# A sketched-attention and top-2 expert kernel: a router with other steps, one row tile for both halves of batch 0, and the first block's rows turned earlier in the program

## The chip, the cores and the metric

The kernel runs on one core of one Trainium2 chip. A core has TensorE (PE, whose weight loads the profile shows apart as PEld), VectorE (DVE), ScalarE (ACT), GpSimd (POOL) and SyncE (SP), each with a queue of its own that it works off in order. The metric is the device time of one execution in microseconds; the time of a kernel is the median of its runs. The kernel before took 388.87 us (three runs, 386.61 to 390.64).

## The reference

Four batches of 1088 tokens, four heads of 32, float32. A sketch turns every key and query head into 64 features, the attention is linear in them, and its result (4352 tokens by 128) goes through a noisy top-2 router to eight experts of 128 x 1024 x 128:

```python
a, b = x @ S1.T, x @ S2.T                  # 8 numbers each, per head and token
phi = outer(a, b).reshape(64)
kv, z = phi(k).T @ v, phi(k).sum(0)
x = (phi(q) @ kv) / (phi(q) @ z + 1e-6)    # heads side by side: (4352, 128)
noisy = x @ w_gate + log1p(exp(x @ w_noise)) * noise
top2 = the two largest of the 8 per token; w = softmax over the two
out = sum over the two of w * (relu(x @ w1[e]) @ w2[e])
```

## The kernel before, in words

**Stages.** A batch is eight tiles of 128 tokens; the 64 tokens left over of two batches share a ninth tile, so routers 0 to 3 have 8, 9, 8 and 9 tiles. `Features` makes the features of up to four tiles: `turn` transposes on PE and copies on ACT, `sketch` multiplies by the sketch on PE and has ACT copy one part out of PSUM, `multiply` adds the other part from PSUM (L363) and forms the outer product (L368), both on DVE, the product on POOL where that is asked for. `keys_values` (L404) sums keys times values in one PSUM bank, `through_router` (L418, L424) folds the router's weights in, `Attend` (L444, L461) gives numerators, denominators and raw logits in a tile `nd`.

**Router.** `router` (L471) is a generator of small DVE steps, one a `yield`: divide, add up the heads, softplus, noise, then twice over maximum, compare, rank, pick; then prefix sums over the tiles, and on PE three small matmuls (L561 to L563) count how many earlier tokens chose each expert. With the start of the expert's area (`base`) this gives the row `to` of each token's two copies. The token, times its weight, goes into a tile `xg` (L586), and one indirect DMA for each tile and choice (L603, POOL) scatters 128 rows of it to `xs` in DRAM. `xg` has two buffers. Batch 0 is routed as two halves, `h0` and `h1`, of four tiles, each with an `xg` of its own; their steps alternate on DVE, by the counts in `both(n)`.

**Blocks.** `table` works out on DVE which expert and which rows each block of 128 rows has (`making` in the code). `work_off` goes through 72 blocks: it fetches a block's weights (L750) and rows (L758) on SP, turns the rows on PE (L762), and multiplies by w1 (L816) and w2 (L773) in two halves; ACT or DVE applies the relu, POOL scatters the results (L780). Blocks come in waves of 9, 18, 16 and 29; a wave's rows can be fetched when its batch's scatters have landed. Within the waves each further half block is one `next` on the generator, and the work of later batches lies between them.

**What sets the order.** On PE, ACT and DVE the order is that of the program (`manual_schedule`). The orders of POOL and SP are set by the framework's scheduler, which places an instruction by when it believes it ready; so a step that stands later in the program can stand earlier there. `first_batches` writes the order up to the first blocks out by hand: batch 0 (tiles `k0`, `k1`, `kr`, `q0`, `q1`), batch 1's keys `l0`, `l1` and queries `p0`, `p1`, `pr`, batch 2's keys `m0`, `m1`, `mr`. Then come the steps of router 1, and between them batch 2's `keys_values`; the first `next` on the blocks is after `LONE` = 2 yields of `routing(1)`, which cover twelve router steps and half of batch 2's `keys_values`, and after six more steps and its other half.

Of the kernel before, what the change touches and what calls it, by code (L numbers as in the profile page):

```python
# [11 lines left out]
ALU = mybir.AluOpType  # L12
# [9 lines left out]
def kernel(  # L22
# [192 lines left out]
    base = const.tile([P, E], F32, name="base")  # L215
    for e in range(E):
        nc.gpsimd.memset(base[:, e:e + 1], float(e * CAP))
# [15 lines left out]

    carry = [const.tile([P, E], F32, name="carry0")]
    nc.gpsimd.memset(carry[0][:], 0.0)
# [94 lines left out]
    class Features:  # L330
# [14 lines left out]
        def sketch(self):  # L345
            n, ps = self.n, early_bank(self.b, self.stream)
            for i in range(n):
                nc.tensor.matmul(ps[:, P * i:P * (i + 1)], lhsT=self.xT[:, P * i:P * (i + 1)],  # L348
                                 rhs=sk[:].rearrange("p i h y -> p (i h y)"), start=True, stop=True)
            self.two = ps[:, 0:P * n].rearrange("p (a i b y) -> p a i b y", a=n, i=2, b=H)  # L350
            self.ab = work.tile([P, G, H, 2, R], F32, name="ab", tag=f"ab{self.stream}",
                                bufs=3 if self.stream == "k" else 2)
            self.o = self.ab[:, 0:n].rearrange(
                "p a b w r -> p b a (w r)" if self.by_head else "p a b w r -> p a b (w r)")
            nc.scalar.copy(self.o, self.two[:, :, 1])  # L355

        def multiply(self, engine=V):
            for _ in self.products(engine):
                pass

        def products(self, engine=V):
            n = self.n
            yield V.tensor_tensor(out=self.o, in0=self.two[:, :, 0], in1=self.o, op=ALU.add)  # L363
            if self.phi is None:
                self.phi = work.tile([P, G, H, RR], F32, name="phi", tag=f"phi{self.stream}",
                                     bufs=3 if self.stream == "q" else 2)
            th = self.ab[:, 0:n].rearrange("p t h w r -> p (t h) w r")
            yield engine.tensor_tensor(  # L368
                out=self.phi[:, 0:n].rearrange("p t h (i j) -> p (t h) i j", i=R),
                in0=th[:, :, 0, :].unsqueeze(3).to_broadcast([P, H * n, R, R]),  # L370
                in1=th[:, :, 1, :].unsqueeze(2).to_broadcast([P, H * n, R, R]), op=ALU.mult)
# [97 lines left out]
    marks = []  # L469

    def router(nd, at_, n, t0, step, part, parts):  # L471
# [21 lines left out]
        yield V.tensor_add(out=sc[:, :, 0:2, :], in0=sc[:, :, 0:2, :], in1=sc[:, :, 2:4, :])  # L493
        lz = t3("lz", 2 * E)
        yield V.tensor_add(out=lz, in0=sc[:, :, 0, :], in1=sc[:, :, 1, :])
# [12 lines left out]
        yield V.reciprocal(up, up)  # L508
        yield V.tensor_mul(out=c, in0=c, in1=up)
# [7 lines left out]
        rk = rank[:].unsqueeze(1).to_broadcast([P, n, E])  # L517
        first = small.tile([P, 2, MOST, E], F32, name="first", tag="first")
        top, pick = [], t1("pick")
# [3 lines left out]
        for i in range(2):  # L523
            m = t1(f"m{i}")
            yield V.tensor_reduce(out=m, in_=noisy, axis=AX.X, op=ALU.max)
            if i == 1:
                yield V.tensor_sub(out=g2, in0=m, in1=top[0])
                nc.scalar.activation(out=g2, in_=g2, func=AF.Exp)
            yield V.tensor_tensor(out=c, in0=noisy, in1=wide(m), op=ALU.is_equal)
            yield V.tensor_mul(out=c, in0=c, in1=rk)  # L530
            yield V.tensor_reduce(out=pick, in_=c, axis=AX.X, op=ALU.max)
            yield V.tensor_tensor(out=first[:, i, 0:n, :], in0=c, in1=wide(pick), op=ALU.is_equal)
            if i == 0:
                yield V.scalar_tensor_tensor(out=noisy, in0=first[:, 0, 0:n, :], scalar=-2e38, in1=noisy,
                                             op0=ALU.mult, op1=ALU.add)
            top.append(m)
# [17 lines left out]
        if step == B - 1:  # L554
# [10 lines left out]
        yield V.tensor_scalar(out=g1, in0=g2, scalar1=1.0, scalar2=1e-9, op0=ALU.add, op1=ALU.add)  # L565
        yield V.reciprocal(g1, g1)
        yield V.tensor_mul(out=g2, in0=g2, in1=g1)
        co = small.tile([P, 2, MOST, H], F32, name="co", tag="co")
        yield V.tensor_tensor(
            out=co[:, :, 0:n], in0=den.rearrange("p t a h -> p t (a h)").unsqueeze(1).to_broadcast([P, 2, n, H]),  # L570
            in1=g[:, :, 0:n].unsqueeze(3).to_broadcast([P, 2, n, H]), op=ALU.mult)
        row = t3("row")
        yield V.tensor_tensor(out=row, in0=o, in1=base[:].unsqueeze(1).to_broadcast([P, n, E]), op=ALU.add)
        of = small.tile([P, 2, MOST, E], F32, name="of", tag="of")[:, :, 0:n]
        yield V.tensor_tensor(out=of, in0=first[:, :, 0:n], in1=row.unsqueeze(1).to_broadcast([P, 2, n, E]), op=ALU.mult)
        to_f = small.tile([P, 2, MOST], F32, name="to_f", tag="to_f")[:, :, 0:n]
        yield V.tensor_reduce(out=to_f, in_=of, axis=AX.X, op=ALU.add)
        to = small.tile([P, 2, MOST], U32, name="to", tag="to", bufs=3)
        yield V.tensor_copy(to[:, :, 0:n], to_f)
        send_all(step)  # L580
        xg = moe.tile([P, 2, MOST, XW], F32, name="xg", tag="xg", bufs=2)
        nc.gpsimd.tensor_copy(xg[:, :, 0:n, D:XW].bitcast(I32), pair[:, :, t0:t0 + n].unsqueeze(3))

        for i in range(2):
            for hp in range(2):
                yield V.tensor_tensor(  # L586
                    out=xg[:, i, 0:n, 2 * DH * hp:2 * DH * (hp + 1)].rearrange("p t (h d) -> p t h d", h=2),
                    in0=x[:, :, hp, 0:2 * (DH + 2)].rearrange("p t (h y) -> p t h y", h=2)[:, :, :, 0:DH],
                    in1=co[:, i, 0:n, 2 * hp:2 * hp + 2].unsqueeze(3).to_broadcast([P, n, 2, DH]), op=ALU.mult)
            for t in range(n):  # L590
                waiting.append((step, i, t, to, xg))
            if step == 0:
                send(n)
# [26 lines left out]
    V.memset(taken[:], 0.0)  # L620
# [12 lines left out]
    def table(step, K, last):  # L633
# [27 lines left out]
        yield V.tensor_add(out=start[:, 0:E], in0=base[0:1, :], in1=taken[:])  # L661
# [44 lines left out]
        if last:  # L706
            yield V.tensor_tensor(out=tab[:, 0, K:K + E], in0=cnt, in1=base[0:1, :], op=ALU.add)
# [27 lines left out]
    def work_off(*waves, skip=0, most=None, at=None):  # L735
# [70 lines left out]
        turn_input(0, acc)  # L806
        for b in range(n):
# [71 lines left out]
    LONE = 2  # L879
# [47 lines left out]
    def first_batches():  # L927
# [18 lines left out]
        V.tensor_copy(number[:], count_i[:])  # L946
        V.tensor_scalar(out=number_p[:], in0=number[:], scalar1=float(P), scalar2=None, op0=ALU.mult)
# [28 lines left out]
        some(h0, 5)  # L976
# [5 lines left out]
        l0.sketch()  # L982
        both(6)
        l1.sketch()
        p0.turn()
        both(8)
        p1.turn()
        p0.sketch()
        both(7)
        both(2)  # L990
        p1.sketch()
        both(3)
# [3 lines left out]
        l0.multiply()  # L996
# [4 lines left out]
        next(making)  # L1001
        values = keys_values(1)
# [61 lines left out]
    def routing(b, nd):  # L1064
# [8 lines left out]
        def fill():  # L1073
            if b + 1 < B:
                yield from keys_values(b + 1)
# [33 lines left out]
    with tc.manual_schedule(engines={PE, ACT, DVE}):  # L1109
        nd = first_batches()  # L1110
        steps_ = routing(1, nd)
        some(steps_, LONE)
        needs = [0]
        blocks = block_work(*range(B), most=-SPARE, at=needs)

# [55 lines left out]
```

## Time and profile before

| what | value |
|---|---|
| median of three runs | 388.87 us |
| the profiled execution | 392.52 us |
| its span, first to last instruction | 390.8 us |
| PE busy | 360.4 us (92%), 3022 matmul records |
| DVE, ACT, POOL busy | 153.5, 124.6, 153.5 us |
| granted PE clock, mean | 0.954 |
| scatters of tokens (L603) | 68, 1035 ns each |
| first block's rows turned (L762) | at 70.25 us |

The profile has one page for one execution: busy time, the span in forty slices with the granted PE clock, DMA queues, the chain of waits that ended last, and groups of instructions by line with what ended the idle time before them. The trace can also be asked for a timeline, for who waited for whom, and for the busy time in any stretch. Times in the text are microseconds from the start of the span. A matmul record of float32 with 128 columns takes 0.11 us of PE at full clock and 0.21 us at half.

### The profile page before, as it was taken

Reading aid. Unit: us, or ns where it says so; the run is one execution under the profiler, and the core shown is the slowest. Engines: PE = TensorE matmul, PEld = TensorE weight load, DVE = VectorE, ACT = ScalarE, POOL = GpSimd, SP = SyncE. Lnnn points to the kernel's source line nnn. Section 1 sums busy time; section 2 is a strip of 40 time slices with the busy share of each in tenths; the row PEclk is TensorE's granted clock in tenths of the full one; section 3 lists DMA queues with packets and bytes.
Section 4 is the critical chain, followed back from the end, with each engine's and each line's share of the span. In section 5 each row is a group of like instructions: output and inputs, shape, how many; then the busy total and the mean of one; then the engine's idle time right before and its main releaser. Section 6 shows DMA issues by size and latency. Waiting matters only on the chain.

```text
span 390.8 us, 9212 instructions
## 1 busy us (share of the span) xinstructions
PE 360.4 (92%) x3022; PEld 351.3 (90%) x3022; DVE 153.5 (39%) x490; ACT 124.6 (32%) x310; POOL 153.5 (39%) x206
## 2 busy tenths in 40 slices
PE   8987797999899997998999999999999999999980
PEld 8886686999799997998999999999999999998980
DVE  5869634844245450057710232232232232343330
ACT  3352142455334443543443222222212212212110
POOL 6103662058572174254455555522222222323230
PEclk9999666999999996999999999999999999999995
DMA  6799734246216363365668876665655655979623
GB/s 188 185 298 292 223 104 158 107 146 167 87 56 202 96 204 103 85 174 158 187 181 196 261 196 200 212 167 181 196 160 186 193 166 180 386 275 319 177 67 86
DMA packets 45742, 70.38 MB, mean 180 GB/s; under 512 B 9971, under 2 KB 31092, under 8 KB 45696
## 3 DMA queue, kind: packets, MB, share of 16 engines
q1 hardware_dynamic: 36784, 58.47, 51.6%
q0 software_dynamic: 4480, 8.96, 6.6%
q10 hardware_dynamic: 4432, 2.36, 2.0%
q8 instruction: 27, 0.44, 0.5%
q14 instruction: 19, 0.16, 0.1%
HBM read 57.99 MB, written 12.03 MB: 179 GB/s over the span
## 4 chain that ended last, share of the span: by engine, by line
PE 78%; DMA 10%; issue 4%; another core or an unknown queue 3%; DVE 2%; ACT 1%; POOL 1%; POOLq 0%; DVEq 0%; ACTq 0%
PE hp L816 29%; PE acc L773 28%; DMA parts<-y,xb 8%; PE bank L404 4%; PE bank L348 3%; PE bank L461 2%; PE acc L461 2%; PE acc L762 2%; PE acc L444 2%; PE bank L341 1%; DMA w<-in_moe_w_dram 1%; PE side L925 1%; PE bank L444 1%; DMA two<-parts 1%
## 5 line engine op out<-in xcount | busy, mean ns | idle before, releaser
L816 PE MATMUL hp<-bT,w 128*128 128x128 f32 x1152 | 154.7, 277 | 1.4 <-issue 0.9
L773 PE MATMUL acc<-w,h 128*128 x1152 | 153.0, 276 | 1.0 <-issue 1.0
L816 PEld LDWEIGHTS hp<-bT,w 128*128 128x128 f32 x1152 | 141.0, 193 | 2.4 <-issue 0.9
L773 PEld LDWEIGHTS acc<-w,h 128*128 128x128 f32 x1152 | 141.0, 193 | 1.8 <-issue 1.8
L780 POOL DMA_INDIRECT parts<-y,xb x72 | 73.9, 1026 | 172.6 <-DVE y L731 89.0
L733 ACT ACTIVATE h<-hp 128x512 f32<-128x512 f32 x99 | 59.2, 598 | 146.8 <-PE hp L816 114.0
L603 POOL DMA_INDIRECT xs<-xg,to x68 | 70.4, 1035 | 43.1 <-DVE xg L586 22.7
L731 DVE TENSOR_SCALAR h<-hp 128x512 f32<-128x512 f32 x45 | 31.1, 692 | 122.5 <-PE hp L816 107.9
L733 ACT COPY bT<-acc 128x128 f32<-128x128 f32 x72 | 19.2, 266 | 32.7 <-PE acc L762 17.3
L762 PE MATMUL acc<-ident,xb 128*128 128x128 f32 x72 | 19.8, 275 | 2.0 <-ACT y L733 1.3
L404 PE MATMUL bank<-vld,phi 128*128 128x96 f32 x128 | 18.7, 313 | 1.3 <-DVE phi L368 0.8
L404 PEld LDWEIGHTS bank<-vld,phi 128*128 128x128 f32 x128 | 18.2, 229 | 1.6 <-DVE phi L368 0.9
L368 DVE TENSOR_TENSOR phi<-ab 128x1024 f32<-128x1024 f32 (+1 forms) x17 | 19.2, 1131 | 0.6
L731 DVE COPY y<-acc 128x128 f32<-128x128 f32 x45 | 13.1, 292 | 11.7 <-PE acc L773 11.5
L348 PE MATMUL bank<-sk,xT 128*128 128x128 f32 x102 | 15.5, 305 | 1.2 <-ACT xT L343 1.2
L348 PEld LDWEIGHTS bank<-sk,xT 128*128 128x128 f32 x102 | 14.0, 215 | 2.3 <-ACT xT L343 2.1
L363 DVE TENSOR_TENSOR ab<-bank,ab 128x256 f32<-128x256 f32 (+1 forms) x15 | 5.6, 375 | 24.9 <-ACT ab L355 23.1
L762 PEld LDWEIGHTS acc<-ident,xb 128*128 128x128 f32 x72 | 10.3, 144 | 2.6 <-ACT y L733 1.7
L486 DVE TENSOR_SCALAR den<-nd 128x16 f32<-128x16 f32 (+2 forms) x5 | 0.9, 179 | 29.1 <-issue 24.3
L461 PE MATMUL bank<-kv,phT 128*128 128x98 f32 (+1 forms) x72 | 10.1, 307 | 2.4 <-ACT phT L449 2.4
L461 PEld LDWEIGHTS bank<-kv,phT 128*128 128x128 f32 (+1 forms) x72 | 9.5, 216 | 2.7 <-ACT phT L449 2.6
L586 DVE TENSOR_TENSOR xg<-nd,co 128x256 f32<-128x256 f32 (+2 forms) x20 | 10.9, 606 | 0.5 <-DMA parts<-y,xb 0.2
(185 smaller groups left out, 247.4 us busy)
## 6 DMA issues: line engine op xcount, KB each, us to landing
w<-in_moe_w_dram SPq DMA_DIRECT2D x72, 512.0 KB
xb<-xs SPq DMA_DIRECT2D x72, 64.5 KB
two<-parts SPq DMA_DIRECT2D x7, 512.0 KB
kld<-in_k_dram SPq DMA_DIRECT2D x4, 512.0 KB
qld<-in_q_dram SPq DMA_DIRECT2D x4, 512.0 KB
vld<-in_v_dram SPq DMA_DIRECT2D x8, 256.0 KB
out_dram<-two ACTq DMA_DIRECT2D x7, 256.0 KB
parts<-y,xb POOLq DMA_INDIRECT x72
```

The costliest lines, as they stand in the source:

```text
L348: nc.tensor.matmul(ps[:, P * i:P * (i + 1)], lhsT=self.xT[:, P * i:P * (i + 1)], rhs=sk[:].rearrange("p i h y -> p (i h y)"), start=True, ...
L368: yield engine.tensor_tensor(out=self.phi[:, 0:n].rearrange("p t h (i j) -> p (t h) i j", i=R), in0=th[:, :, 0, :].unsqueeze(3).to_broadca ...
L404: nc.tensor.matmul(ps[:, W * hp:W * (hp + 1)], lhsT=lhsT, rhs=rhs, start=(t == 0 and hp == 0), stop=(t == NT), skip_group_check=True)
L444: nc.tensor.transpose(ps[:, P * i:P * (i + 1)], self.part.two_heads(i, hp), ident[:])
L461: nc.tensor.matmul(ps[rows, c0:c0 + YC], lhsT=self.phT[hp][:, P * i + rows.start:P * i + rows.stop], rhs=kv[:, hp, :], start=True, stop=True)
L603: x = nc.gpsimd.indirect_dma_start(out=xs[:], out_offset=bass.IndirectOffsetOnAxis(ap=to[:, i, t:t + 1], axis=0), in_=xg[:, i, t, :], in_o ...
L731: V.tensor_scalar_max(o, i, 0.0) if relu else V.tensor_copy(o, i)
L733: nc.scalar.activation(out=o, in_=i, func=AF.Relu) if relu else nc.scalar.copy(o, i)
L762: nc.tensor.transpose(acc[:, P:2 * P], rows[i][:, 0:D], ident[:])
L773: nc.tensor.matmul(acc[:, 0:D], lhsT=h[:, P * j:P * (j + 1)], rhs=w2[:, bass.ds(FJ * e + (j0 + j), 1), :], start=(j0 + j == 0), stop=(j0 + ...
L780: sent = nc.gpsimd.indirect_dma_start(out=parts[:], out_offset=bass.IndirectOffsetOnAxis(ap=rows.pop(i)[:, D:XW].bitcast(U32), axis=0), in ...
L816: nc.tensor.matmul(hp[:, P * j:P * (j + 1)], lhsT=w1[:, P * (j0 + j):P * (j0 + j + 1)], rhs=xT[:], start=True, stop=True)
```

## The change

1. *Router steps.* The two additions of heads become one reduction. The two largest values come from `V.max`, one instruction a tile, and the two compare-rank-pick rounds share the compare and the ranking, as one instruction of twice the width each. `base` is gone: the first carry starts at e*CAP/128 in each partition, so the counting matmuls give the row at once, which `of` reads from PSUM; `to` is written by a reduction with a whole-number output, without a conversion of its own. The weights are worked out before the prefix sums, the first choice's rows (`weighted(0)`) before `to`. With four tiles the router has 41 steps in place of 44, with nine tiles 48 in place of 46.
2. *One tile for both halves of batch 0.* `h0` and `h1` write halves of one `xg`.
3. *`l0`.* ACT copies both parts of `l0`'s sketch out of PSUM, and POOL does both the addition and the product, ahead of most of batch 0's router in the program.
4. *First block.* `work_off` yields after it has fetched and turned the first block's rows. That first `next` now stands directly after half of batch 2's `keys_values`, ahead of router 1 and of the loads of batch 3, and `LONE` is 1.
5. Two small conversions for the tables (`number`, `number_p`) move from before `q0.multiply` to after the first step of table 0; the counts in `both` are adapted.

```diff
+    for e in range(E):
+        nc.gpsimd.memset(carry[0][:, e:e + 1], float(e * CAP // P))
...
             nc.scalar.copy(self.o, self.two[:, :, 1])
+            self.part0 = self.two[:, :, 0]
+            if apart:
+                t = work.tile([P, G, H, 2, R], F32, name="ab", tag=f"ab{self.stream}", bufs=3)
+                self.part0 = t[:, 0:n].rearrange("p a b w r -> p b a (w r)")
+                nc.scalar.copy(self.part0, self.two[:, :, 0])
...
-            yield V.tensor_tensor(out=self.o, in0=self.two[:, :, 0], in1=self.o, op=ALU.add)
+            yield add.tensor_tensor(out=self.o, in0=self.part0, in1=self.o, op=ALU.add)
...
-        yield V.tensor_add(out=sc[:, :, 0:2, :], in0=sc[:, :, 0:2, :], in1=sc[:, :, 2:4, :])
-        yield V.tensor_add(out=lz, in0=sc[:, :, 0, :], in1=sc[:, :, 1, :])
+        yield V.tensor_reduce(out=lz, in_=sc.rearrange("p t h y -> p t y h"), axis=AX.X, op=ALU.add)
...
+        for t in range(n):
+            yield V.max(out=most[:, t, :], in_=noisy[:, t, :])
+        yield V.tensor_sub(out=g2, in0=most[:, :, 1], in1=most[:, :, 0])
+        nc.scalar.activation(out=g2, in_=g2, func=AF.Exp)
+        yield V.tensor_tensor(out=same, in0=noisy..., in1=most[:, :, 0:2]..., op=ALU.is_equal)
+        yield V.tensor_mul(out=same, in0=same, in1=rank...)
+        yield V.tensor_reduce(out=pick, in_=same[:, 0], axis=AX.X, op=ALU.max)
+        yield V.tensor_tensor(out=first[:, 0, 0:n, :], in0=same[:, 0], in1=wide(pick), op=ALU.is_equal)
+        yield V.tensor_scalar(out=g1, in0=g2, scalar1=1.0, scalar2=1e-9, op0=ALU.add, op1=ALU.add)
+        yield V.scalar_tensor_tensor(out=same[:, 1], in0=first[:, 0, 0:n, :], scalar=-float(E), in1=same[:, 1], ...)
+        yield V.reciprocal(g1, g1)
+        yield V.tensor_reduce(out=pick, in_=same[:, 1], axis=AX.X, op=ALU.max)
+        yield V.tensor_mul(out=g2, in0=g2, in1=g1)
+        yield V.tensor_tensor(out=first[:, 1, 0:n, :], in0=same[:, 1], in1=wide(pick), op=ALU.is_equal)
+        yield V.tensor_tensor(out=co..., in0=den..., in1=g..., op=ALU.mult)
+        if part == 0:
+            shared["xg"] = moe.tile([P, 2, MOST, XW], F32, name="xg", tag="xg", bufs=2)
+        xg = shared["xg"][:, :, at_:at_ + n] if step == 0 else shared["xg"]
...
-        yield V.tensor_tensor(out=row, in0=o, in1=base..., op=ALU.add)
-        yield V.tensor_tensor(out=of, in0=first..., in1=row..., op=ALU.mult)
-        yield V.tensor_reduce(out=to_f, in_=of, axis=AX.X, op=ALU.add)
-        yield V.tensor_copy(to[:, :, 0:n], to_f)
+        for hp in range(2):
+            yield weighted(0, hp)
+        yield V.tensor_tensor(out=of, in0=first..., in1=o..., op=ALU.mult)
+        yield V.tensor_reduce(out=to[:, :, 0:n], in_=of, axis=AX.X, op=ALU.max)
...
         turn_input(0, acc)
+        yield
...
-        l0.sketch()
+        l0.sketch(True)
+        l0.multiply(nc.gpsimd, nc.gpsimd)
...
-        l0.multiply()
         m0.turn()
         l1.multiply()
...
-        steps_ = routing(1, nd)
-        some(steps_, LONE)
         needs = [0]
         blocks = block_work(*range(B), most=-SPARE, at=needs)
+        values = keys_values(2)
+        some(values, NG)
+        next(blocks)
+        steps_ = routing(1, nd, values)
+        some(steps_, LONE)
```

## Prediction before the run

> **What bounds the kernel now.** I read the page first, slices and chain. From slice 8 on (about 70 us) PE is busy in nearly every tenth, and its clock is full but for one dip.
>
> ```profile
> PE   8987797999899997998999999999999999999980
> PEclk9999666999999996999999999999999999999995
> ...
> PE hp L816 29%; PE acc L773 28%; DMA parts<-y,xb 8%; PE bank L404 4%; PE bank L348 3%; PE bank L461 2%; PE acc L461 2%; PE acc L762 2%; PE acc L444 2%; PE bank L341 1%; DMA w<-in_moe_w_dram 1%; PE side L925 1%; PE bank L444 1%; DMA two<-parts 1%
> ```
>
> Blocks (L816, L773, L762) are PE work, 72 x 33 records x 0.11 us = 265 us, and nothing here shortens it. What the change can move is when the first block starts: any shift of it moves the end, as long as PE stays the bound behind it. So I asked for the chain up to 90 us.
>
> ```profile
> 36.46 8.66 another core or an unknown queue
> ...
> 58.51 1.86 issue
> ...
> 65.00 5.25 PE bank L404 x32
> 70.25 0.12 PE acc L762
> ```
>
> PE reaches block 0's turn at 70.25, coming straight from batch 2's `keys_values` (L404 x32, 0.16 us a record, so half clocked). Were the rows there? The timelines of SP and POOL:
>
> ```profile
> 54.58 2.25 SPq L750 DMA_DIRECT2D w<-in_moe_w_dram  x3
> 64.06 2.01 SPq L758 DMA_DIRECT2D xb<-xs  x3
> ```
>
> ```profile
> 35.33 1.19 POOL L603 DMA_INDIRECT xs<-xg,to  x1 [21.46 <-DVE xg L586]
> ...
> 46.05 0.96 POOL L603 DMA_INDIRECT xs<-xg,to  x1 [0.30 <-issue]
> 50.36 0.21 POOL L582 COPY xg<-pair 128x18 int32<-128x18 int32 x1 [3.35 <-DMA xs<-xg,to]
> 51.11 0.98 POOL L603 DMA_INDIRECT xs<-xg,to  x1 [0.54 <-POOL xg L582]
> ...
> 60.52 0.96 POOL L603 DMA_INDIRECT xs<-xg,to  x1 [0.30 <-issue]
> ```
>
> Rows are asked for at 64.06, 2.6 us after the last of batch 0's 16 scatters ended (61.48), and can be used about 2 us later (an estimate: block 9's rows were asked for at 118.55 and turned at 121.24), at 66. So two paths meet at block 0: the scatters, 66, and PE's own work, 70. The second decided in this execution, by 4 us. It holds two kinds of loss: half clock (the stretches 46 to 52 and 62 to 68 show a granted clock of 0.50) and waits. POOL stood 3.8 us between the eighth and ninth scatter, since `xg` for batch 1 (L582) needs the buffer of `h0`.
>
> [...] half-clock stretches follow the idle ones at 43 to 45.6 and 58 to 61. [...] 34 elements that took as long as POOL's product:
>
> ```profile
> 11.95 1.95 DVE L947 TENSOR_SCALAR number_p<-number 1x34 f32<-1x34 f32 x1
> ```
>
> ```profile
> 11.92 1.95 POOL L368 TENSOR_TENSOR phi<-ab 128x1024 f32<-128x1024 f32 x1 [4.08 <-DVE number L946]
> ```
>
> No DVE instruction with two SBUF inputs meets a long POOL reader in this trace. [...] I price a `max` as the smallest pipelined step, 0.1 us.
>
> **The change, part by part.**
>
> *Router steps, batch 0.* The halves alternate on DVE, so a small step costs its issue interval, 0.11 us (28.56, 28.68, 28.79, ...), not its 0.19 us latency; fewer dependent steps save only issue slots. For each half: two rounds of twelve steps (1.3 us) become eight small and double-width ones plus four `max` (0.94 + 0.4); two adds (0.29 + 0.23) become one reduction of 256 elements (0.42); `row` (0.11) and the conversion (0.2) go. But `h1` now has four more steps (g1, reciprocal, g2, `co`) ahead of `h0`'s scatter, 0.44. Sum: about -0.1 us for the first scatter, -0.4 to +1.0 with `max` at 0.08 to 0.25. Router 1 stands alone (0.265 us a step): nine `max` +0.9, shared rounds level, `row`, conversion and overlapped weights -1.3, reduction -0.2: -0.6. It is hidden: blocks follow PE's order, and the router's rows are needed only as blocks complete.
>
> *One `xg` tile.* Batch 1's L582 gets the free buffer: the 3.8 us gap goes. Scatters then run 16 in a row: 11.7 (first eight) + 0.3 + 10.4 = 22.4 us, 0.7 more if L582 falls among them.
>
> *`l0` on POOL.* DVE loses 0.45 + 1.2 = 1.65 us, though behind `h0`'s rows, so that no scatter gains from it. POOL needs 1.95 for the product and about 0.6 for the addition (a quarter of the elements), from about 27.6, when ACT's second copy (0.37) is done, to 30.2. DVE is then in the router[...]. I take 2.4. That shifts `h0`'s counting inputs (31.7 before; they also come after `co` now) to about 34.7. `p1.sketch` queues behind L561 on PE, harmless, but PE is idle from 30 to 34.7[...].
>
> *Scatters.* Ready 34.4 - 0.1 + 2.4 = 36.7, first at 37.6, last ends at 60.0 to 60.7, rows asked for at 63.3, usable at 65.3: 0.7 us earlier than before.
>
> *PE.* `l1.multiply` runs from about 37.5 to 39.1 on DVE (before 36.6 to 38.2). It frees the bank of batch 1's `keys_values` at 37.9 and completes its input. Before, that stage went from 36.7 to 45.1, when ACT was let go, at half clock and with 2.4 us that the records don't explain. Now it starts near 39 with nearly all input there: 36 records x 0.11 = 4.0 us at full clock, to 43.2, or x 0.21, to 46.7. From there the chain took 25 us to the turn; at full clock without the unexplained waits I count 16. Starting at 43.2 gives 59.5 to 68.2, then the rows at 65.3 decide or nearly. [...] Either way the turn, so corrected, comes at about 67.7: gain 2.5 us. With 46.7 + 25 = 71.7 it is a loss of 1.5.
>
> *First `next`.* One PE turn stands at the same place as before, behind half of `keys_values`; twelve router steps in place of eighteen lie before the first L816, on DVE, which isn't late. Three weight and two row fetches with their table loads now precede batch 3's four loads (1.5 MB) in the program. SP issued those at 41.9 to 45.2, ahead of the fetches, and I expect it to again; behind the row wait they would land near 72, and batch 3's keys are turned at 90.8: 0. Router 1's two further steps give one more half block before batch 2's scores. That moves 16 records (1.8 us) past block 9's turn, whose rows came 0.6 us early: 0 to +1.3, I take 0.
>
> *Small ones.* `number` and `number_p`, 0.3 us on DVE ahead of `p0`, whose features had PE time to spare; the extra memsets (0.03 each) fall in POOL's idle 8 to 11.9; ACT's copy lies in a gap.
>
> Sum for the profiled execution: 392.5 - 2.5 = 390.0. It lies 3.65 above the median of the runs; against the median the same shift gives 388.87 - 2.5 = **386.4**.
>
> **Rivals.**
> *No port block:* scatters begin at 35.2, end near 58, rows are usable at 62.7, PE's chain is 2.4 earlier and warm: 70.2 - 62.7 = 7.5 less 2.5 of half clock is 5: 383.9. For it: no two-input case is in the trace. Against: the 1.95 us of L947.
> *Cold chain:* PE idles from 30 to 34.7, falls to half clock and stays so: turn at 71.7, and block 9 waits 1.3: 388.87 + 2.8 = 391.7. For it: half of 44 to 70 was cold before.
> *Slower, the shared tile as a wait:* if `h1`'s row writes on DVE wait for `h0`'s scatters to land (37.6 + 11.7 + 2 = 51.3 in place of 39.5), `p0`, table and `p1` queue behind on DVE, `p0`'s features come at 55 where PE wants them at 45: turn at 68.2 + 10 = 78, so 397. It decides from a wait of about 2 us on. For it: L582 did wait for landings. Against: DVE wrote the second choice's rows (L586, 33.63 on, 1.42 us unbroken) into a tile in which POOL writes too.
>
> **Numbers.** Chances: 0.40 main, 0.30 no port block, 0.20 cold chain, 0.10 shared tile. Less than 1% (3.9 us) is about what a measurement can't tell from no change. The main case spans 384 to 389, a fifth of it below 385; nearly all of the second is faster; a third of the third is slower. Faster 0.37, same 0.46, slower 0.17. The range reaches from 381.5, the second with a warm start, to 392.5, the cold chain's end, and leaves out the shared tile; the main case's own range is 384 to 389.
>
> **What would show it.** POOL: no wait in L582, 16 scatters in a row from 37.6 (no block: 35.2) to 60. DVE: steps of over 0.5 us at 28 to 30 beside POOL's L368. PE: L404 for batch 1 done near 43, turn at 65 to 68, clock at half in fewer slices before 70. Wrong if DVE waits for a DMA before L586, if POOL puts `l0` behind scatters, or if block 9 waits for over 2 us.

## The result and the profile after

The changed kernel takes 399.27 us (median of four runs, 398.50 to 400.73). The kernel before took 389.05 beside it (four runs, 386.61 to 390.64). The ratio is 1.0273, 95% interval 1.0211 to 1.0335: slower by 2.7%, where I had forecast 386.4 us and put the end of the range at 392.5. The profiled execution took 400.73 us, its span is 398.9 us. Ratios here and below leave disturbed runs out (over 1.5% above the fastest of the same kernel), medians hold all runs, and the traces of `e8` and `e11` are of disturbed runs.

The page's slices show a kernel that idles more at its start and does the same work afterwards (rows of PE and of its granted clock; compare with the rows of before in the prediction):

```profile
PE   8985958997599999899999999999999999997980
...
PEclk9996677998899999999999999999999999998996
```

The timelines of POOL and DVE, 27 to 31 us, are the ones in which I had announced DVE steps of over 0.5 us beside POOL's L368. A line has start, duration, engine, line, operation and tiles, and in brackets the engine's idle time before it and what ended it; for `issue` and `remote` the profile names no engine that did.

```profile
27.43 0.76 POOL L368 TENSOR_TENSOR ab<-ab 128x256 f32<-128x256 f32 x1 [13.77 <-ACT ab L360]
28.27 1.95 POOL L373 TENSOR_TENSOR phi<-ab 128x1024 f32<-128x1024 f32 x1
```

```profile
27.54 0.71 DVE L518 TENSOR_TENSOR noisy<-sp,noise 128x32 f32<-128x32 f32 x1
28.17 0.34 DVE L513 RECIPROCAL ur<-up 128x32 f32<-128x32 f32 x1
28.43 1.83 DVE L519 TENSOR_TENSOR noisy<-noisy,lz 128x32 f32<-128x32 f32 x1
30.19 0.18 DVE L514 TENSOR_TENSOR c<-c,ur 128x32 f32<-128x32 f32 x1
```

Two steps that take 0.19 us when POOL does nothing (L518 at 30.92, L519 at 31.15) last 0.71 and 1.83: DVE loses 2.2 us, beside POOL's two instructions and ending with them (at 28.25 and 30.26; POOL's end at 28.19 and 30.22). PE's timeline shows what follows (the first line is of the kernel before): the counting matmuls (L589, L561 in the kernel before) come at 34.10 in place of 31.27, and batch 1's keys times values (L409, L404 before) runs at half clock, 32 records in 7.13 us (granted clock 0.51 in the mean from 40.5 to 47.7). But the first block's turn (L776) comes only 2.4 us later than before:

```profile
31.27 0.41 PE L561 MATMUL side<-sums,earlier 128*128 128x32 f32 x2 [1.33 <-DVE sums L540]
```

```profile
34.10 0.64 PE L589 MATMUL side<-sums,earlier 128*128 128x32 f32 x2 [4.39 <-DVE sums L568]
...
40.56 7.13 PE L409 MATMUL bank<-vld,phi 128*128 128x96 f32 x32
...
55.50 2.03 PE L466 MATMUL acc<-kv,phT 128*128 128x98 f32 x8 [1.46 <-issue]
59.77 5.21 PE L466 MATMUL acc<-kv,phT 128*128 128x98 f32 x24 [2.25 <-issue]
...
72.45 0.27 PE L776 MATMUL acc<-ident,xb 128*128 128x128 f32 x1
```

The rest comes later. The n-th turn in the two traces, counted from 0: turn 0 at 70.08 and 72.45, turn 4 at 86.98 and 88.67, turn 6 at 98.37 and 107.68. So between turns 4 and 6 the changed kernel falls 7.6 us further behind. (The trace of before has a dip of its own, some 7 us between turns 14 and 15, and the changed kernel one near its end, where PE waits 2.61 us for rows at 363.75; so the end of the two traces says less than these places.) In that stretch PE waits for ACT (4.06 us until 104.40), and ACT for releases of PE, the semaphore updates that say that its matmuls are done. Those at 94.73 and 102.08 come 1.9 and 1.7 us after the last matmul recorded before them ends (92.84 and 100.34); such ends the profile models and doesn't measure. ACT's lines, with waits of 2.08 to 2.62 us:

```profile
94.76 0.27 ACT L747 COPY y<-acc 128x128 f32<-128x128 f32 x1 [2.30 <-remote]
97.10 0.60 ACT L747 ACTIVATE h<-hp 128x512 f32<-128x512 f32 x1 [2.08 <-remote]
...
102.17 0.60 ACT L747 ACTIVATE h<-hp 128x512 f32<-128x512 f32 x1 [2.62 <-remote]
```

It is also where batch 1's scatters begin. Router 1's counting matmuls stand behind five half blocks in place of three, at 84.43 in place of 75.63 (first the line of the kernel before, then that of the changed one), and its first scatter starts at 87.50 in place of 81.59:

```profile
75.63 0.34 PE L561 MATMUL side<-sums,earlier 128*128 128x72 f32 x2
```

```profile
84.43 0.34 PE L589 MATMUL side<-sums,earlier 128*128 128x72 f32 x2
```

```profile
58.22 0.96 POOL L616 DMA_INDIRECT xs<-xg,to  x1 [0.30 <-issue]
62.49 0.21 POOL L556 COPY xg<-pair 128x16 int32<-128x16 int32 x1 [3.31 <-DMA xs<-xg,to]
81.49 1.07 POOL L794 DMA_INDIRECT parts<-y,xb  x1 [18.78 <-ACT y L747]
87.50 0.96 POOL L616 DMA_INDIRECT xs<-xg,to  x1 [4.95 <-DVE xg L560]
```

The first of POOL's lines is batch 0's last scatter. It ends at 59.2, 2.3 us earlier than before (forecast: 60.0 to 60.7). The second is batch 2's `xg`.

### The profile page after: what moved, and what is told of

Same layout as the page of the kernel before. It is cut to its first block, busy times and chain, and to the rows that moved or that the text cites. A ratio compares the mean times of both kernels' runs of the same rounds, so it can differ in the third digit from the quotient of the medians.

```text
span 398.9 us, 9213 instructions
## 1 busy us (share of the span) xinstructions
PE 362.0 (91%) x3022; PEld 353.3 (89%) x3022; DVE 150.7 (38%) x486; ACT 124.7 (31%) x311; POOL 156.5 (39%) x215
## 4 chain that ended last, share of the span: by engine, by line
PE 75%; DMA 11%; issue 5%; DVE 5%; ACT 1%; POOL 1%; another core or an unknown queue 1%; POOLq 0%; DVEq 0%; ACTq 0%
PE hp L831 28%; PE acc L787 27%; DMA parts<-y,xb 9%; PE bank L409 4%; PE acc L466 3%; PE bank L348 3%; PE bank L466 2%; PE acc L776 2%; PE bank L340 1%; DMA w<-in_moe_w_dram 1%; PE acc L449 1%; PE side L940 1%; PE hp L348 1%; DMA two<-parts 1%; POOL parts L794 1%
## 5 line engine op out<-in xcount | busy, mean ns | idle before, releaser
L794 POOL DMA_INDIRECT parts<-y,xb x72 | 73.1, 1016 | 178.8 <-DVE y L745 89.3
L787 PEld LDWEIGHTS acc<-w,h 128*128 128x128 f32 x1152 | 142.6, 195 | 0.0
L747 ACT ACTIVATE h<-hp 128x512 f32<-128x512 f32 x99 | 59.2, 598 | 152.1 <-PE hp L831 113.7
L616 POOL DMA_INDIRECT xs<-xg,to x68 | 71.3, 1048 | 31.4 <-issue 19.8
L747 ACT COPY bT<-acc 128x128 f32<-128x128 f32 x72 | 19.1, 265 | 33.9 <-PE acc L776 20.4
L776 PE MATMUL acc<-ident,xb 128*128 128x128 f32 x72 | 20.0, 278 | 5.6 <-DMA xb<-xs 2.6
L409 PE MATMUL bank<-vld,phi 128*128 128x96 f32 x128 | 18.5, 312 | 0.1
L409 PEld LDWEIGHTS bank<-vld,phi 128*128 128x128 f32 x128 | 17.9, 227 | 0.3 <-DVE of L533 0.3
L368 DVE TENSOR_TENSOR ab<-bank,ab 128x256 f32<-128x256 f32 (+1 forms) x14 | 5.2, 370 | 33.5 <-ACT ab L355 33.5
L776 PEld LDWEIGHTS acc<-ident,xb 128*128 128x128 f32 x72 | 10.4, 144 | 6.5 <-issue 5.5
L466 PE MATMUL acc<-kv,phT 128*128 128x98 f32 (+1 forms) x72 | 12.0, 339 | 4.2 <-issue 3.7
L466 PEld LDWEIGHTS acc<-kv,phT 128*128 128x128 f32 (+1 forms) x72 | 11.0, 245 | 5.1 <-issue 4.2
L348 PE MATMUL bank<-sk,xT 128*128 128x128 f32 x102 | 13.5, 280 | 1.5 <-ACT xT L342 0.8
L348 PEld LDWEIGHTS bank<-sk,xT 128*128 128x128 f32 x102 | 12.2, 192 | 2.6 <-ACT xT L342 2.4
L747 ACT COPY y<-acc 128x128 f32<-128x128 f32 x27 | 7.2, 267 | 13.8 <-PE acc L787 7.7
```

Source lines behind the costliest of these rows:

```text
L409: nc.tensor.matmul(ps[:, W * hp:W * (hp + 1)], lhsT=lhsT, rhs=rhs, start=(t == 0 and hp == 0), stop=(t == NT), skip_group_check=True)
L466: nc.tensor.matmul(ps[rows, c0:c0 + YC], lhsT=self.phT[hp][:, P * i + rows.start:P * i + rows.stop], rhs=kv[:, hp, :], start=True, stop=True)
L616: x = nc.gpsimd.indirect_dma_start(out=xs[:], out_offset=bass.IndirectOffsetOnAxis(ap=to[:, i, t:t + 1], axis=0), in_=xg[:, i, t, :], in_o ...
L747: nc.scalar.activation(out=o, in_=i, func=AF.Relu) if relu else nc.scalar.copy(o, i)
L776: nc.tensor.transpose(acc[:, P:2 * P], rows[i][:, 0:D], ident[:])
L787: nc.tensor.matmul(acc[:, 0:D], lhsT=h[:, P * j:P * (j + 1)], rhs=w2[:, bass.ds(FJ * e + (j0 + j), 1), :], start=(j0 + j == 0), stop=(j0 + ...
```

## The experiments

I began with four theories. *A*: POOL's work on `l0` holds DVE, PE idles and goes cold. *B*: router 1's counting is late, so batch 1's scatters fall on blocks 4 to 9. *C*: the losses at turns 4 to 7 are accidents of the clock. *D*: the new order around the first block costs by itself. A fifth, *S*, came out of the runs `e1` to `e12`. All ratios are against the kernel before on the same chip in the same hours; its median was 387.6 to 390.4 us, except beside `e17` and `e18`.

### One part undone, or one part alone

`e1`: the changed kernel with

```diff
-        l0.sketch(True)
-        l0.multiply(nc.gpsimd, nc.gpsimd)
+        l0.sketch()
...
+        l0.multiply()
         m0.turn()
```

> The changed kernel with l0's addition and product back on DVE at their old place behind h0; nothing else is undone and nothing is left out. Theory A (POOL's work on l0 holds DVE, PE idles 4.4 us and goes cold): DVE's counting inputs at about 32 in place of 34.1, first scatter at about 34.5 in place of 36.6, block 0's turn at 69 to 70.5 in place of 72.45, median 394 to 396.5 in place of 399.3. Theory B (the counting matmuls of router 1 stand behind five half blocks in place of three, so batch 1's scatters are 6 us later and the loss falls in blocks 4 to 9): the turn may move, but the stalls between turns 4 and 7 stay, median 397 or more. Theory C (the losses at turns 4 to 7 are accidents of the clock): the median follows block 0's turn alone, 396 to 397.

Measured: 1.0209 (1.0132 to 1.0287), median 395.4. Counting at 31.86 and the first scatter at 35.0, as A says, and yet the turn at 74.33, later than in the changed kernel. The wait had moved: batch 1's keys times values ran from 37.3 to a recorded end at 41.7, and ACT was let go at 49.6.

`e2`: the kernel before with this part alone.

> The kernel before with one part of the change alone: l0's addition and product on POOL, placed right behind its sketch. Theory A: DVE steps of 1.8 us and 0.7 us beside POOL's two, h0's counting matmuls 2 us later than 31.7, first scatter near 37.3 in place of 35.3, block 0's turn at 72 to 73 in place of 70.2, median 391 to 394 in place of 389. Theory B: no more than the 0 to 2 us of that shift, and no further loss at turns 4 to 7. If the whole loss of 10 us is an effect of the cold start alone, 397 or more.

Measured: 1.0177 (1.0097 to 1.0256), the dearest of the four parts. The turn comes at 74.47, 4.4 us later than before and twice the 2.2 us that DVE lost beside POOL in the changed kernel; in the trace the distance is 7.6 us at turn 7 and 4.5 at the end.

`e3`, for theory B:

```diff
-            some(steps_, 5)
+            some(steps_, 8)
```

> The changed kernel with eight router steps in place of five between two half blocks, for routers 1 to 3, so that the counting matmuls of router 1 again stand behind three half blocks on PE as in the kernel before (five in the changed one). Theory B: counting at 78 to 80 in place of 84.4, batch 1's first scatter at 82 or earlier in place of 87.5, the stalls at turns 4 to 7 shrink, median 393 to 396. Theory A: block 0's turn stays at 72.45 and the median at 397 to 400, since DVE isn't what blocks wait for. More steps in one piece could also delay DVE's share of the relu: then 400 or more.

Measured: 1.0184 (1.0104 to 1.0265), median 394.6. Counting at 79.2, as B says, but the first scatter at 85.2, where B wanted 82 or earlier. Some 0.9% is gained; the two intervals overlap.

`e4`: the old order around the first block in the changed kernel (`LONE = 2`, `routing` ahead of it, no `yield` behind `turn_input`).

> The changed kernel with the order around the first block as before: no yield behind the first block's turn, router 1's first steps and batch 3's loads ahead of it, LONE 2. Counting stands behind four half blocks. Theory A: 398 to 400, no change. Theory B: half of the late counting goes, batch 1's first scatter at 85 to 86, median 396 to 398. Theory D (batch 3's value load, which the changed kernel puts between the second and third row fetch on SP, and the earlier turn are what costs): all of the loss past block 0's turn goes, median 391 to 393.

Measured: 1.0172 (1.0098 to 1.0247), median 395.4. That is not D's 391 to 393. It lies below B's 396 to 398 too, but B's mechanism isn't in the trace: counting stands at 83.97 and the first scatter at 87.05, nearly as late as in the changed kernel, and the turn comes at 76.19. What gave the 1.0% is open; here too the intervals overlap.

`e5`: `e1` and `e3` together.

> The changed kernel with both edits of the two runs that gained about half each: l0 on DVE at its old place, and eight router steps between two half blocks, so that router 1's counting matmuls stand behind three half blocks again. If the two costs are independent and add up (l0 on POOL 4 to 5 us, late counting 4 to 5 us), the median comes to 389 to 391, level with the kernel before. If both edits only took away one and the same loss (a start that is late by any means), it stays at 394 to 396. If it is below 387, the shared tile or the earlier first turn brings a gain that the other two parts hid.

Measured: 1.0145 (1.0100 to 1.0191), turn at 73.76. The gains of `e1` and `e3`, 0.6 and 0.9%, add up to this within the intervals, but A and B together leave half of the loss.

The three other parts, each alone on the kernel before (`e6`: the router's steps; `e7`: one row tile; `e8`: the order around the first block):

> The kernel before with the new router steps alone: two row tiles, l0 on DVE, the first block, the two small conversions and LONE as before. Counting stands behind four half blocks in place of three. Theory B (late counting): 1.5 to 3 us slower than before, 390.5 to 392. If the reduction, the nine maximum steps and the later counting of h0 cost nothing and the lateness is hidden: 388 to 389.5. If the new steps carry all that is left of the loss: 394 or more.

> The kernel before with one row tile for both halves of batch 0 and no other edit. The gap of 3.8 us between the eighth and the ninth scatter goes, the last of the 16 ends at 57 to 58 in place of 61.5, rows are asked for at about 60. As recorded, PE's own work reaches block 0's turn only at 70, so the median stays at 387 to 391. If PE's work is held by the scatters or by what runs beside them, it moves by more than 2 us: faster if the end of the scatters sets it, slower if their density does (393 or more). If DVE waited for scatters in the shared tile: 395 or more.

> The kernel before with the new order around the first block alone: the first rows fetched and turned behind half of batch 2's keys times values, then a pause, then router 1 and batch 3's loads, LONE 1. Counting stands behind four half blocks in place of three, at 77.5 in place of 75.6. Theory B: 1 to 3 us slower, 390.5 to 392. As I had predicted: no difference, 388 to 390. Theory D (this order by itself costs the loss past block 0's turn): 393 or more.

Measured: `e6` 1.0081 (1.0052 to 1.0111), turn at 73.14. `e7` 1.0032 (0.9992 to 1.0071), turn at 74.01. `e8` 0.9998 (0.9960 to 1.0036), turn at 71.32. DVE waited for no scatter in `e7`. D falls: this order alone costs nothing. `e8` also speaks against B: its counting stands behind four half blocks in place of three (79.50 and 75.63), and it is no slower, where B expected 1 to 3 us. C is not settled: `e1`, whose counting comes at 86.30, loses nothing between turns 4 and 6, but 5.8 us between turns 6 and 8. Taken alone the four parts sum to 2.9%, about the whole loss; the two small conversions were not tried alone.

### The cold clock

`e9` puts idle matmuls into PE's gap ahead of h0's counting, `e10` the same kind at two places of the kernel before, `e12` at all three places of the changed kernel:

```diff
         p0.sketch()
+        keep_warm(18)
         both(10)
```

> The changed kernel with 18 idle matmuls (36 records, 4.0 us at full clock) put on PE ahead of h0's counting matmuls, in the 4.4 us in which PE waits for DVE there; they write a bank that nothing reads. Theory A's second half (the idle gap makes PE cold from 33.9 to 47.5 and that is what costs): the clock stays full past 34, batch 1's keys times values runs in 4 us in place of 7.7, block 0's turn comes at 69 to 70 in place of 72.45, median 395 to 397. If the half clock there is hidden behind other waits: 398 to 400, no change. If the filler delays the counting matmuls: 400 or more.

> The kernel before with eight idle matmuls at each of two places where PE stood idle: behind batch 1's keys times values (idle 42.8 to 45.6) and ahead of the last attention tile (idle 58.5 to 60.4). Nothing else is changed. If cold windows bound the start: the half clock of 44.6 to 54.8 and 61.6 to 68.4 shrinks[...], block 0's turn at 66 to 68, median 386 to 388 in place of 390.4. If PE's work there is held by releases that come late whatever the clock: 389 to 392.

> The changed kernel with the idle matmuls at all three places of the two runs beside it: 18 ahead of h0's counting, eight behind batch 1's keys times values, eight ahead of the last attention tile. If the cold windows between 30 and 68 us carry the half of the loss that shows as half clock (about 8 us more of it in a run, worth 4 us): half clock in a run falls to 30 us or less, median 394 to 396. If it is merely filled with work that does nothing: 398 or more.

Measured: `e9` 1.0243 (1.0178 to 1.0309), `e10` 1.0080 (1.0048 to 1.0113), `e12` 1.0293 (1.0244 to 1.0343). The filler did its work. In `e9` the 32 records of keys times values took 3.81 us in place of 7.13, and ACT copied the sums at 42.35, 6 us earlier than in the changed kernel. Still the turn came at 75.41. The mean granted clock of the profiled execution is 0.950 in `e9`, 0.966 in `e12` and 0.949 in the changed kernel; in `e10` it is 0.977, before it was 0.954. ACT's timeline of `e9` shows where the 6 us went:

```profile
42.35 0.21 ACT L414 COPY kv<-bank 64x66 f32<-64x66 f32 x1 [3.79 <-issue]
...
48.33 0.18 ACT L432 COPY kv<-bank 64x32 f32<-64x32 f32 x1
...
59.99 0.87 ACT L469 COPY nd<-acc 128x392 f32<-128x392 f32 x2 [5.11 <-remote]
```

A stage that was 6 us early, and batch 1's numerators (L469, L464 in the kernel before) leave PSUM at 60.0, as in the changed kernel, where it was 60.6. So the half clock at this place is not what costs. The last wait, 5.11 us, is for PE's matmuls L466, the only work that this copy reads; they are recorded as ended by 57.0.

`e11`: the changed kernel without `l0` on POOL and without the new order, so router and row tile together.

> The changed kernel without its two other parts: l0 back on DVE, the old order around the first block. What is left of the change are the router's steps, the shared row tile and the two small conversions. If the parts' costs add up (router steps alone +0.8%, shared tile alone +0.3%): 393 to 395. If the shared tile costs nothing beside the router: 392 to 394. If the parts don't add up, and any one of them spoils the start: 395 to 397, as with three other mixtures of them.

Measured: 1.0171 (1.0104 to 1.0237), turn at 75.52. The two alone sum to 1.1%, which the interval still holds.

### The pause between the scatters

So the parts alone would make up the whole, but undoing one or two of them gives back only 0.6 to 1.3%, and the turn is late in nearly all. I sorted the traces by what POOL does. In the kernel before, POOL's order has eight scatters, then batch 1's `xg` (L582), which waits, then eight more: a pause of 4.1 us. The scheduler sets this order, and nearly any edit changes it: in the changed kernel and in `e1` to `e7`, `e9`, `e11` and `e12`, all 16 scatters stand in one row, though `e2` and `e6` still have two row tiles. Only `e8` and `e10` kept the pause.

| kernels | pause | numerators leave PSUM from | first block's turn |
|---|---|---|---|
| before, `e8`, `e10` | 3.7 to 4.6 us | 51.4 to 55.2 | 69.0 to 71.3 |
| changed, `e1` to `e7`, `e9`, `e11`, `e12` | none | 55.5 to 64.2 | 72.4 to 76.2 |

Each kernel stands here with a single trace, and the rows touch: `e6`, without a pause, has its first numerators at 55.5, the kernel before at 55.2. This is theory *S*: in an unbroken row of scatters PE's releases come late, and in the pause the chain of small stages gets through. `e14`, `e15` and `e16` put the pause back (in `e16`: 4.65 us in place of 4.10) in the changed kernel, in `e7` and in the kernel before, by a later place of h1's last steps:

```diff
         next(values)
         next(values)
         next(values)
-        all_of(h1)
...
         pr.multiply()
+        all_of(h1)
```

> The changed kernel with one edit: h1's last steps (its rows, its row numbers) stand behind the multiply of batch 1's last queries on DVE, so that batch 0's scatters again run as eight, a pause of 4 to 6 us from about 47 on, and eight. Theory S: batch 1's numerators leave PSUM at 51 to 58 in place of 60.6 to 66.8, block 0's turn at 69 to 70.5 in place of 72.45, median 395 to 396.5 in place of 399.3. If what sets the turn is PE's clock[...]: 398 to 400. If the rows of block 0, which come 4 us later, decide: 400 or more.

> The kernel before with the shared row tile alone, and the pause put back in the same way. Theory S: the turn at 70 in place of 74.0, median level with the kernel before (within 1 us of it), that is 2 to 3 us below the mean of the run with the shared tile alone. If the shared tile costs by itself, 392 or more whatever the pause.

> The kernel before, whose pause between the eighth and the ninth scatter was 4.1 us, with h1's last steps moved back in the same way, so that the pause is some 6 us. Theory S: batch 1's numerators leave PSUM by 56, PE's work reaches block 0's turn at 67 to 69, but rows are asked for at 66 and can be used at 68: median 387 to 390, level or 1 us better. If later rows decide: 391 or more.

Measured: `e14` 1.0193 (1.0158 to 1.0227), median 395.3; `e15` 0.9987 (0.9951 to 1.0023), median 387.7; `e16` 1.0027 (0.9996 to 1.0058). The numerators leave from 55.0, 51.1 and 49.5, the turns come at 69.59, 66.92 and 67.27: all three below every kernel without a pause. POOL's and ACT's timelines of `e7`, then of `e15`, which differ in the pause and in DVE's h1 steps that move with it:

```profile
46.14 0.96 POOL L606 DMA_INDIRECT xs<-xg,to  x1 [0.30 <-issue]
47.40 0.96 POOL L606 DMA_INDIRECT xs<-xg,to  x1 [0.31 <-issue]
```

```profile
59.07 0.87 ACT L464 COPY nd<-acc 128x392 f32<-128x392 f32 x2 [5.19 <-remote]
```

```profile
45.84 0.96 POOL L606 DMA_INDIRECT xs<-xg,to  x1 [0.30 <-issue]
52.77 0.96 POOL L606 DMA_INDIRECT xs<-xg,to  x1 [5.97 <-issue]
```

```profile
51.12 0.49 ACT L464 COPY nd<-acc 128x392 f32<-128x392 f32 x1 [0.73 <-PE acc L461]
52.01 0.49 ACT L464 COPY nd<-acc 128x392 f32<-128x392 f32 x1 [0.41 <-PE acc L461]
```

Scatters eight and nine start 1.26 us apart in `e7`, 6.9 in `e15`. With the pause the numerators follow each other every 0.9 us; without it the first waits 5.19 us for a release. In time the two kernels differ by 0.45%, and their intervals overlap.

No run has the pause put back without h1's steps moved, and the pause can't be all: that of `e16` is hardly longer than before, and that of `e10` is 4.62 us, yet the numerators of `e16` leave 5.7 us earlier than before. ACT copies batch 1's sums in `e16` at 42.81 in place of 45.14, when the pause (from 46.7 on) has not begun. So the new place of h1's steps on DVE is a rival to S, and it was not tested.

The turn no longer tells of PE's own work in these kernels. PE is ready early and waits for the rows, which come when the second eight scatters have landed (in `e14` the last of them ends on POOL at 66.29, POOL's wait for landings at 67.77, and the rows are asked for at 67.83); the lines are of `e14` and of `e16`, and in `e15` the wait is 5.28 us:

```profile
69.59 0.47 PE L776 MATMUL acc<-ident,xb 128*128 128x128 f32 x1 [3.76 <-DMA xb<-xs]
```

```profile
67.27 0.47 PE L762 MATMUL acc<-ident,xb 128*128 128x128 f32 x1 [7.53 <-DMA xb<-xs]
```

From ACT's copy of the sums to the place where PE is ready for the turn it takes 17.6, 17.2 and 16.9 us in `e14`, `e15` and `e16`, and 24.9 before. `e16` is no faster for it.

In the changed kernel the pause gives back 0.8%, about 3 us; the two intervals just overlap. Where these 3 us lie the trace doesn't say: the turn is 2.9 us earlier than in the changed kernel, but turn 4, at 88.12, only 0.55, and turn 6, at 107.90, not at all. The first turn is earlier than in the trace of before, and `e14` is still 1.9% slower.

### The hand-off by itself, and all together

`e13` and `e17` leave the whole computation out and measure hand-offs from PE to ACT and back alone: 

```python
for j in range(4):
    nc.tensor.matmul(ps[:, P * j:P * (j + 1)], lhsT=ident[:], rhs=x[:, P * j:P * (j + 1)], start=True, stop=True)
nc.scalar.copy(x[:], ps[:])
```

> A kernel that measures the disputed cost by itself and leaves the whole computation out: 112 hand-offs in a chain, each four 128 x 128 matmuls on PE and one 128 x 512 copy on ACT, and the output filled with zeros. After 16 hand-offs POOL starts 16 token scatters (128 rows of 516 bytes, indirect) one behind the other; after 32 more, 16 plain transfers of the same bytes from POOL; after 32 more, SP loads eight times 0.5 MB. Theory S (PE's releases come late while scatters follow each other without a gap): hand-offs take about 1.8 us alone and 3 us or more beside the scatters, with single ones of 3 to 6 us, and 1.8 us again from the end of the scatters on. If it is transfers in general that do it: the same beside the plain transfers or the loads. If hand-offs are no slower in any stretch, theory S falls.

> The chain of hand-offs measured by itself again, with the whole computation left out and the output filled with zeros. Each of three trains of 16 scatters now has company: the first eight loads of 0.5 MB on SP, the second eight loads in pieces of 128 bytes, the third 24 multiplications of 128 x 1024 on DVE. Alone a hand-off took 2.81 us, and beside scatters without company 3 of 8 took 3.1 to 3.8. If scatters and loads together are what holds PE's releases: hand-offs of 4 us or more beside the first or second train, none beside the third. If DVE's use of SBUF does it: beside the third. If none is over 4 us, the holds of 3 to 6 us in the kernel have a cause that these four measurements don't contain, and it stays open.

Measured: a hand-off takes 2.81 us. In `e13` two beside the scatters took 3.82 and 3.53, none beside the plain transfers; two more, behind the scatters and behind the loads, took 3.1. (The expectation of `e17` counts one of these among the first.) In `e17` none beside any of the three trains took more than 2.81. So neither run shows waits as long as the kernel's: what holds PE's releases isn't reproduced, and S's mechanism stays unshown. `e17` also ran on the chip of `e18`, whose trace shows next to none of these waits, so it says little of the other chips.

`e18`: the changed kernel with `l0` on DVE, eight steps a half block and the pause.

> The changed kernel with three edits at once: l0 on DVE, eight router steps between two half blocks, and the pause of about 6 us between batch 0's eighth and ninth scatter. The first two together gave 396.1 in the mean. Theory S: the pause takes off another 4 us, block 0's turn at 67 to 69 in place of 73.8, median 390 to 393 and, on this chip's scale, within 1% of the kernel before. If the pause no longer helps, because other waits take its place: 395 or more.

Measured: 0.9971 (0.9946 to 0.9997), turn at 64.93. Level with the kernel before, or 0.3% faster, and the fastest ratio of all; it keeps the router's steps, the row tile and the new first `next`. But `e17` and `e18` ran on a chip on which the kernel before took 379.2 us, and not 387.6 to 390.4. The semaphore events of its one trace of the kernel, `e18`, differ too. In the trace of before, PE's releases come in bursts after a silence of over 1.2 us (two to five within 0.1 us of each other, where matmuls of a group are 0.9 us long) at 14 places, in the changed kernel at 12, in `e1` to `e16` without `e13` at 10 to 19. In `e18` there is one, at 364. These counts need care, since the record is not whole: in the trace of before it has 404 updates of the 467 that PE's instructions make, 381 of DVE's 443 and 244 of ACT's 295, and in `e18` all 467 of PE's. So a silence can in part be a gap in the record, and what is late need not be PE's alone; ACT's waits are measured apart from it. On that chip the kernel with the three edits is level with the kernel before. Whether the whole change loses anything there, whether the chip or the edits ended the silences, and whether the edits would do on the other chips, was not tried.

## Why the prediction was wrong

*What bounds the kernel.* "Any shift of it moves the end, as long as PE stays the bound behind it" failed. The turn moved by 2.4 us and the median by 10.2, and between turns 4 and 6 PE waited for ACT; in `e7` the turn came 3.9 us later, with a ratio of 1.0032, and in `e16` 2.8 us earlier, with 1.0027. (The 265 us of the blocks need 0.1115 us a record, the mean from start to start at full clock in the trace; with 0.11 they are 261. Nothing hangs on it.)

*Router steps, batch 0.* The size was about right, as was its irrelevance for the first scatter: `e6` starts it at 35.1, before it was 35.3. (The terms as listed sum to about 0, not -0.1.) The reduction was mis-sized, 0.60 us for 128 x 256 in place of 0.42.

*Router 1, "It is hidden".* Wrong. I counted the time of its steps, not their number: 48 steps at five a half block move the counting matmuls on PE, in the order of the program, from behind three half blocks to behind five. So it isn't hidden; whether it costs is open. `e3`, which undoes it, takes off 0.9%, with intervals of 0.6 and 0.8% each way, and in `e8`, with counting behind four half blocks, no cost is measured.

*One `xg` tile.* The gap went, the row ended at 59.2 (forecast 60.0 to 60.7), rows were asked for at 62.55 (63.3). All right, but I booked the gap as a loss alone. PE's chain may have got through in it (theory S, not shown); closing it alone cost 0.3%, not clear of no change (`e7`).

*`l0` on POOL.* Right: DVE's loss beside POOL's two instructions was taken as 2.4 us, an estimate, and measured as 2.2; counting at 34.7 forecast, 34.10 measured. L519's 1.83 us beside POOL's 1.95, in place of 0.19, puts *No port block* out, the rival in which DVE loses nothing there. By what POOL holds DVE, no run shows. That *l0* costs 1.8% alone isn't explained by these 2.2 us, and the rest is open; the edit also removed the pause.

*PE.* This is the step that failed first, and it gave the forecast its sign: "From there the chain took 25 us to the turn; at full clock without the unexplained waits I count 16." I let the unexplained waits go because I saw no cause, and a wait without a known cause is the last that may be counted as gone. The chain took 24.1 us in the changed kernel (48.34 to 72.45), 24.9 before (45.14 to 70.08); the lines are ACT's copy of the sums before and after:

```profile
45.14 0.21 ACT L409 COPY kv<-bank 64x66 f32<-64x66 f32 x1 [8.69 <-remote]
```

```profile
48.34 0.21 ACT L414 COPY kv<-bank 64x66 f32<-64x66 f32 x1 [7.16 <-PE bank L409]
```

It didn't shrink either when the stage before it took 3.81 us in place of 7.13 (`e9`: 42.35 to 75.41). The count of 16 itself was nearly right: `e14` to `e16`, where the waits are gone, took 16.9 to 17.6, and then the rows decided, about 2 us after they were asked for, as the prediction has it (67.83 and 69.59 in `e14`). With 25 us in place of 16 the forecast is the *cold chain*, 391.7. The other 7.6 us of the 399.27 are the second failure, the terms behind the turn that I put at nothing ("It is hidden", "I take 0"): in the trace 7.6 us go between turns 4 and 6, and which of these terms they belong to stays open.

*First `next`.* "I take 0" held alone (`e8`, 0.9998). It gives one of the two half blocks by which counting is late; the router's further steps give the other.

*Rivals.* *Cold chain* came nearest: PE idled 4.39 us, its granted clock fell to 0.50 at 33.9 and stayed there until 47.5, the stage ran at half clock as priced. The cost of that isn't what I thought: with fillers in the gaps the time stayed (1.0243 and 1.0293). The half clock that the prediction charges behind a wait for rows, in its turn at 67.7 and with 2.5 us in *No port block*, was an estimate; measured is the record of the turn, 0.47 us behind the waits of `e14` and `e16` (3.76 and 7.53 us), 0.27 in the changed kernel (72.45). *Shared tile as a wait* is false: no step of DVE waited for a scatter.

What stays open: what holds PE's releases, why it hardly shows in the one trace from the fourth chip, and what the 1.9% left in `e14` are. That scatters cause it is argued from 17 traces and three edits that also move DVE's work; it is not shown.

## What to carry to other kernels

Never count a wait as gone whose cause you can't name. A milestone that moves need not move the end: check it against the time of several kernels before you forecast by it. Where the scheduler sets an engine's order, compare that order before and after each edit, since an edit elsewhere can change it. And idle time of an engine off the critical path may be time in which another gets through (the first numerators left PSUM at 51.12 in `e15`, with the pause, and at 59.07 in `e7`; that the pause is the cause is not shown), so look at what the others did in a gap before you close it.

## What I had not expected of the hardware

- In the record PE's releases to ACT come late and in bursts. In `e14` four of them, at 102.75, 102.81, 102.87 and 102.93, follow a silence since 98.49, though matmuls that give releases are recorded as ended at 98.86, 99.30 and 99.74. In `e7` one silence lasts 5.8 us. In the trace of `e18`, from another chip, no such burst comes before 364. Part of this can be missing records, but in `e1` ACT really starts 7.9 us after the recorded end of the matmuls that it reads (41.69 and 49.63).
- Removing the half clock of the first blocks' preparation by filler work gained nothing: 1.0243 and 1.0293 with it, 1.0273 without.
- In the changed kernel a `max` of eight elements took 0.16 us (30.51) and nine of them 0.71 us in a row (from 76.16), 0.08 each, where I had taken 0.1.
